# Gated attention followed by two MLP layers on one core: gate sums taken from their middle, masks on a row's last part, row sums in pairs, and one decoding step on another engine

## The chip, the core and the metric

The kernel runs on one core of one Trainium2 chip. The engines are named as the profile names them: PE (matrix products; PEld is its weight load), DVE (vector), ACT (scalar functions), POOL (a third elementwise engine) and SP, whose queue issues all the DMA transfers of this kernel. Each engine works through its own instructions in the order written for it, and waits for others on semaphores. The metric is the device time of one execution in microseconds.

## The reference

Three layers in a row, all in float32:

```python
batch, n_heads, seq, head_dim = (4, 8, 576, 64)
scores = scale * np.matmul(q, k.transpose(0, 1, 3, 2))        # scale = 1/8
causal = np.triu(np.ones((S, S), dtype=bool), k=1)
cum = np.cumsum(np.maximum(s, 0.0), axis=-1)
bias = -(cum[:, :, :, None] - cum[:, :, None, :])
scores = np.where(causal, -1000000000.0, scores + np.minimum(bias, 0.0))
scores = scores - np.max(scores, axis=-1, keepdims=True)
attn = np.exp(scores)
attn = attn / (np.sum(attn, axis=-1, keepdims=True) + 1e-09)
out = np.matmul(attn, v)
...
x = out as [2304, 512]
x = (silu(x @ w_gate) * (x @ w_val)) @ w_out      # 512 -> 1536 -> 512
x = silu(x @ w_in) @ w_out2                       # 512 -> 2048 -> 512
```

A row's softmax doesn't change when a constant is added to the whole row, so of the bias only the part that depends on the key (`cum` at the key) matters to the result.

## The kernel before

**Attention.** There are 32 heads (4 batches of 8). A head's 576 queries are cut into five row tiles, `TILES`, of 64, 128, 128, 128 and 128 rows; a tile's scores reach from key 0 to its last query, so they are 64, 192, 320, 448 and 576 wide. Tiles 0 to 2 are half "A" of a head, tiles 3 and 4 half "B", and a half is a unit. `a_load` issues a head's transfers (`qkr` holds q and k, `cumb` the head's gate sums on all 128 partitions, `vra` and `vrb` the values). `a_split` cuts q and k into a rounded high part (`ks`, `qh`, by `copy`, whose engine letters stand in the strings `KHI` and `QHI`, one letter for each batch: a is ACT, v is DVE, g is POOL) and a remainder (`ql` and the lower rows of `ks`). `a_scores` handles one row tile: POOL writes the gate term into the tile `e` (a `tensor_scalar` over the whole width, L218, then a mask on the diagonal block, `affine_select`, L221), PE makes the scores in PSUM, DVE adds them to `e` and finds the row minimum (`m`, L235), ACT takes the exponential with the row sum `l` (L241), DVE makes `rl` = 1/(l + 1e-9) (L245, L246), and the row is multiplied with it (a `copy`, L114 on DVE or L116 on POOL). `a_transpose` turns the finished rows on PE and `a_pv` multiplies them with the values. There are six `e` tiles, two `cumb` tiles, and five raw weight tiles.

**First MLP layer.** `gate` and `down` work on weight chunks of 2048 columns, nine a batch in the list `L1`. Each product is made three times (`mm3`: high by high, high by low, low by high), so a chunk is 96 matmuls of 288 columns. Weights come as 64-bit words. In the first batch's nine chunks, and in the second layer's eight, `w_decode` has to turn them back to float32, four pieces of 128x512 a chunk: ACT scales the high word (L374), DVE turns the low word to three bits (L375), joins them (L376) and puts the sign in (L379). Later batches read the float32 copy that the first stored. `w_split` then cuts the weights in two parts (`wh` on ACT, `wl` on POOL or DVE, L395).

**Order.** Eighteen units of attention run first, without MLP work, with one chunk's loading and decoding after the ninth. Then the four batches of layer 1 run one after the other, and two units of the next batch's attention are interleaved with each chunk, so that batch 1's attention runs beside batch 0's chunks, while these are being decoded. The fourth batch has no attention beside it. Layer 2 follows. `w_ahead` decodes and splits chunk c+1, and loads chunk c+2, at the start of chunk c. Program order is written so; a scheduler then settles the order on each engine.

## Time and profile before

| | |
|---|---|
| median of 3 runs | 1140.44 us (1138.94 to 1141.12) |
| profiled execution | 1141.18 us, its span 1139.4 us |
| granted PE clock, mean | 0.988 of full speed |
| PE busy | 1096.2 us (96%) |
| DVE busy | 764.8 us (67%) |
| POOL busy | 615.9 us (54%) |
| ACT busy | 561.0 us (49%) |

The span runs from the first to the last instruction; 1.8 us of the execution's time lie outside it. The busy shares are means over stages that differ: the first 76 us are attention alone, then come the four passes of layer 1 (about 76 to 288, 288 to 454, 454 to 615 and 615 to 734 us, read from the first and last matmuls into `pgv` and `po`), then layer 2. Engines take their work in order, so what matters in a stage is the engine that the others wait for there.

### The profile page before, as it was taken

What the parts mean: (1) busy time and instruction counts of PE and PEld (TensorE: products, weight loads), DVE (VectorE), ACT (ScalarE), POOL (GpSimd) and SP (SyncE); (2) the same over time, 40 slices, a digit from 0 to 9 for tenths busy, and PEclk for the clock granted to TensorE, in tenths of its full rate; (3) what the DMA queues carried; (4) which work ended last, traced back from release to release, by engine and by line L of the source; (5) the groups of instructions that cost most, each with busy time, mean ns of one, the idle gap of its engine ahead of it and who ended that gap; (6) DMA issues with size and microseconds to landing.
All of it is one profiled execution on the core that took longest, in us unless ns stands there. A gap on an engine that the chain in (4) does not pass through costs nothing.

```text
span 1139.4 us, 19549 instructions
## 1 busy us (share of the span) xinstructions
PE 1096.2 (96%) x6765; PEld 1000.2 (88%) x6765; DVE 764.8 (67%) x1776; ACT 561.0 (49%) x1242; POOL 615.9 (54%) x731
## 2 busy tenths in 40 slices
PE   7978988989999999999999999999999999999998
PEld 4656888888999999999999999889888898988887
DVE  6888998998877786777766435863463636454333
ACT  5876666655667655576744433455232323322221
POOL 4679889868877776686833543332333232223221
PEclk9988999999999999999999999999999999999999
DMA  5586565666343344333216222630111101000013
GB/s 141 136 244 215 175 193 189 182 173 196 119 119 113 109 117 144 113 101 101 69 54 217 75 84 84 202 109 25 50 51 43 57 19 56 19 1 1 1 51 116
DMA packets 53730, 121.41 MB, mean 107 GB/s; under 512 B 8256, under 2 KB 21568, under 8 KB 53632
## 3 DMA queue, kind: packets, MB, share of 16 engines
q1 hardware_dynamic: 53632, 120.17, 34.6%
q8 instruction: 53, 0.87, 0.3%
q14 instruction: 45, 0.37, 0.1%
HBM read 101.20 MB, written 18.95 MB: 105 GB/s over the span
## 4 chain that ended last, share of the span: by engine, by line
PE 73%; DVE 6%; DMA 2%; issue 2%; ACT 1%; POOL 0%; SPq 0%; DVEq 0%; ACTq 0%
PE po L406 9%; PE po L407 9%; PE po L408 9%; PE pgv L406 7%; PE pgv L407 7%; PE pgv L408 7%; PE pu L407 5%; PE pu L406 5%; PE pu L408 5%; PE pv L292 4%; PE ptr L264 3%; PE psc L230 2%; DVE dk L376 1%; DMA r<-in_w_dram 1%; DMA x2r<-x_d 1%
## 5 line engine op out<-in xcount | busy, mean ns | idle before, releaser
L421 POOL TENSOR_TENSOR h<-u,h 128x288 fp32r<-128x288 f32 (+2 forms) x176 | 187.1, 1064 | 332.5 <-ACT h L112 329.1
L406 PE MATMUL pgv<-xt,wh 128*128 128x288 f32 x768 | 233.7, 305 | 5.0 <-DVE u L417 3.5
L406 PE MATMUL po<-h,wh 128*128 128x288 f32 (+2 forms) x704 | 233.1, 333 | 3.7 <-DVE u L419 1.5
L407 PE MATMUL po<-h,wh 128*128 128x288 f32 (+2 forms) x704 | 232.6, 331 | 0.1
L408 PE MATMUL po<-h,wl 128*128 128x288 f32 (+2 forms) x704 | 232.3, 330 | 0.0
L408 PE MATMUL pgv<-xt,wl 128*128 128x288 f32 x768 | 230.0, 300 | 1.4 <-POOL wl L395 1.4
L407 PE MATMUL pgv<-xt,wh 128*128 128x288 f32 x768 | 230.0, 300 | 0.5 <-DVE xt L313 0.5
L395 POOL TENSOR_TENSOR wl<-wraw,wh 128x1024 fp32r<-128x1024 f32 x53 | 130.0, 2453 | 60.4 <-ACT wh L112 59.9
L406 PEld LDWEIGHTS pgv<-xt,wh 128*128 128x128 f32 x768 | 147.2, 192 | 6.7 <-DVE u L417 4.5
L408 PEld LDWEIGHTS pgv<-xt,wl 128*128 128x128 f32 x768 | 146.7, 191 | 1.8 <-POOL wl L395 1.8
L407 PEld LDWEIGHTS pgv<-xt,wh 128*128 128x128 f32 x768 | 147.1, 192 | 1.1 <-DVE xt L313 0.8
L218 POOL TENSOR_SCALAR e<-cumb,cumq 64x64 f32<-64x64 f32 (+4 forms) x160 | 112.4, 708 | 62.8 <-PE ptr L264 55.2
L406 PEld LDWEIGHTS po<-h,wh 128*128 128x128 f32 x704 | 132.0, 188 | 12.0 <-DVE u L419 2.0
L112 ACT ACTIVATE h<-u 128x288 fp32r<-128x288 f32 (+2 forms) x176 | 88.8, 508 | 102.2 <-DVE u L417 58.5
L408 PEld LDWEIGHTS po<-h,wl 128*128 128x128 f32 x704 | 132.2, 188 | 7.1
L407 PEld LDWEIGHTS po<-h,wh 128*128 128x128 f32 x704 | 132.2, 188 | 6.8 <-POOL h L421 0.5
L241 ACT ACTIVATE e<-e,m 64x64 f32<-64x64 f32 (+4 forms) x160 | 89.2, 558 | 95.9 <-DVE m L235 95.4
L417 DVE SCALAR_TENSOR_TENSOR u<-th,pu 128x464 f32<-128x464 f32 (+1 forms) x80 | 50.5, 631 | 122.3 <-ACT th L415 116.7
L501 DVE SCALAR_TENSOR_TENSOR acc<-po,acc 128x464 f32<-128x464 f32 (+1 forms) x140 | 88.7, 635 | 62.1 <-PE po L408 61.6
L415 ACT ACTIVATE th<-pu 128x464 f32<-128x464 f32 (+1 forms) x80 | 44.2, 552 | 174.0 <-PE pu L408 174.0
L112 ACT ACTIVATE wh<-wraw 128x1024 fp32r<-128x1024 f32 x88 | 92.2, 1053 | 56.0 <-PE po L407 32.1
L407 PE MATMUL pu<-x,wh 128*128 128x464 f32 (+1 forms) x320 | 118.9, 372 | 0.0
(83 smaller groups left out, 2189.3 us busy)
## 6 DMA issues: line engine op xcount, KB each, us to landing
wraw<-w SPq DMA_DIRECT2D x54, 512.0 KB, 4.0
r<-in_w_dram SPq DMA_DIRECT2D x52, 512.0 KB, 5.1
qkr<-in_qk_dram SPq DMA_DIRECT2D x64, 288.0 KB, 4.5
w<-wraw SPq DMA_DIRECT2D x18, 512.0 KB, 4.4
cumb<-cum_d SPq DMA_DIRECT2D x30, 288.0 KB, 3.4
r<-in_w_dram SPq DMA_DIRECT2D x32, 256.0 KB, 3.2
x_d<-acc SPq DMA_DIRECT2D x32, 144.0 KB, 3.8
vrb<-in_vb_dram SPq DMA_DIRECT2D x32, 128.0 KB, 3.6
```

What stands on the lines that cost most here:

```text
L112: nc.scalar.activation(out=out, in_=in_, func=AF.Copy, scale=scale)
L218: nc.gpsimd.tensor_scalar(out=e[:r, :wd], in0=c[:r, :wd], scalar1=-1.0, scalar2=cumq[:r, i, hh : hh + 1], op0=ALU.mult, op1=ALU.add)
L241: nc.scalar.activation(out=e[:r, :wd], in_=e[:r, :wd], func=AF.Exp, bias=m[:r], scale=-1.0, accum_out=l[:r])
L292: nc.tensor.matmul(out=acc[:rows, off : off + width], lhsT=vv, rhs=pp, start=(j == 0 and part == 0), stop=(j == js[-1] and part == len(ps) ...
L395: engines[eng].tensor_tensor(out=wl, in0=t, in1=wh.bitcast(F32), op=ALU.subtract)
L406: nc.tensor.matmul(out=ps[:, :n], lhsT=a, rhs=xh, start=(k == 0), stop=False)
L407: nc.tensor.matmul(out=ps[:, :n], lhsT=a, rhs=xl, start=False, stop=False)
L408: nc.tensor.matmul(out=ps[:, :n], lhsT=c, rhs=xh, start=False, stop=(k == last))
L415: nc.scalar.activation(out=th[:, :n], in_=pg[:, :n], func=AF.Tanh, scale=0.5)
L417: nc.vector.scalar_tensor_tensor(out=u, in0=th[:, :n], scalar=1.0, in1=pg[:, :n], op0=ALU.add, op1=ALU.mult)
L421: engines[LO[ph]].tensor_tensor(out=lo, in0=u, in1=hi.bitcast(F32), op=ALU.subtract)
L501: nc.vector.scalar_tensor_tensor(out=a, in0=ps[:, :n], scalar=0.5, in1=a, op0=ALU.mult, op1=ALU.add)
```

## The change

1. The gate sums are no longer differenced by query. `cum` is centred on the sum at position 288 (`mid`) and multiplied by 8 once; the scores are now made from unscaled q, and L231 multiplies them by -0.125 while it adds the gate. The five transposes and copies to `cumq` at the start are gone.
2. POOL writes no gate term over the whole width any more. It only masks, straight from `cumb`, the part from column `g0` on: all of the row for widths up to 320, and the last 128 or 256 columns of the wider ones. DVE reads the part before `g0` from `cumb` itself. So the tile of width 448 has two DVE additions (320 and 128) instead of one, and the tile of 576 is cut into 320 and 256 instead of 288 and 288.
3. The row sums of tiles 1 and 2, and of tiles 3 and 4, lie in two columns of one tile; 1e-9 and the reciprocal are done once for both, after the second.
4. All rows are now scaled on POOL (`DVE_NORM` is gone; it had put tiles 0, 1 and 3 of batch 0 on DVE).
5. In batch 0, `qh` is made on DVE, not ACT, `ql` on POOL, not DVE, and one of the copies of transposed rows (128x384, half B) moves from ACT to DVE.
6. In `w_decode`, the low word's conversion moves from DVE (L375) to ACT (a second `activation` that writes `dk`).

```diff
+POOL_QL = (0,)
-DVE_PT = ()
+DVE_PT = (("B", 3),)
-QHI = "aavv"
+QHI = "vavv"
-DVE_NORM = [(0, i) for i in (0, 1, 3)]
...
+        mid = sm_p.tile([B * H, 1], F32, tag="m", name="mid")
+        nc.vector.tensor_copy(out=mid, in_=cum[:, HB : HB + 1])
+        nc.vector.tensor_scalar(out=cum, in0=cum, scalar1=mid, scalar2=8.0, op0=ALU.subtract, op1=ALU.mult)
         nc.sync.dma_start(out=cum_d, in_=cum)
-        for i, (q0, r) in enumerate(TILES):
-            pt = ps_a.tile([P, 512], F32, tag="a", name=f"pcum{i}")
-            nc.tensor.transpose(pt[:r, : B * H], cum[:, q0 : q0 + r], ident[: B * H, : B * H])
-            nc.vector.tensor_copy(out=cumq[:r, i, :], in_=pt[:r, : B * H])
...
-            copy(QHI[b], qh[:, q0:k1], t[:, 0, q0:k1], -0.125)
+            copy(QHI[b], qh[:, q0:k1], t[:, 0, q0:k1])
...
-            nc.vector.scalar_tensor_tensor(
-                out=ql[:, q0:k1], in0=t[:, 0, q0:k1], scalar=-0.125, in1=qh[:, q0:k1].bitcast(F32),
-                op0=ALU.mult, op1=ALU.subtract,
-            )
+            eng = nc.gpsimd if b in POOL_QL else nc.vector
+            eng.tensor_tensor(out=ql[:, q0:k1], in0=t[:, 0, q0:k1], in1=qh[:, q0:k1].bitcast(F32), op=ALU.subtract)
...
-        nc.gpsimd.tensor_scalar(
-            out=e[:r, :wd], in0=c[:r, :wd], scalar1=-1.0, scalar2=cumq[:r, i, hh : hh + 1], op0=ALU.mult, op1=ALU.add
+
+        g0 = 0 if wd <= 320 else 320
+        nc.gpsimd.affine_select(
+            out=e[:r, g0:wd], in_=c[:r, g0:wd], pattern=[[-1, wd - g0]], compare_op=ALU.is_ge,
+            fill=-8.0 * QMASK, base=q0 - g0, channel_multiplier=1,
         )
...
+            for g, end, gate in ((c0, min(g0, c0 + n), c), (max(g0, c0), c0 + n, e)):
+                if g >= end:
+                    continue
+                m2 = sm_p.tile([P, 1], F32, tag="m", name="m")
+                nc.vector.tensor_tensor_reduce(
+                    out=e[:r, g:end], in0=ps[:r, g - c0 : end - c0], in1=gate[:r, g:end], scale=-0.125,
+                    scalar=3.0e38 if m is None else m[:r], op0=ALU.add, op1=ALU.min, accum_out=m2[:r],
+                )
+                m = m2
...
-        copy("v" if (b, i) in DVE_NORM else "g", e[:r, :wd], e[:r, :wd], rl[:r])
         st[b, h, "e", i] = e
+        if i in (1, 3):
+            return
+        done = (0,) if i == 0 else (i - 1, i)
+        w = len(done)
+        rl = sm_p.tile([P, 2], F32, tag="rl", name="rl")
+        nc.vector.tensor_scalar(out=l[:r, :w], in0=l[:r, :w], scalar1=1.0e-9, scalar2=None, op0=ALU.add)
+        nc.vector.reciprocal(out=rl[:r, :w], in_=l[:r, :w])
+        for n, j in enumerate(done):
+            q0, r = TILES[j]
+            e = st[b, h, "e", j]
+            copy("g", e[:r, : q0 + r], e[:r, : q0 + r], rl[:r, n : n + 1])
...
-            nc.vector.tensor_scalar(out=k, in0=lo, scalar1=2.0**-29, scalar2=7.0, op0=ALU.mult, op1=ALU.min)
+            nc.scalar.activation(out=k, in_=lo, func=AF.Copy, scale=0.937 * 2.0**-29)
```

The start on DVE, before, from the last copy to `cumq` to the first addition of scores (`ISA e,m`):

```order
L143 COPY cumq<-pcum_146 128x32
L193 TENSOR_TENSOR ks<-qkr,ks 64x576
L194 SCALAR_TENSOR_TENSOR ql<-qkr,qh 128x576
L193 TENSOR_TENSOR ks<-qkr,ks 64x576
L194 SCALAR_TENSOR_TENSOR ql<-qkr,qh 128x576
L235 ISA e,m<-psc,e 64x64
```

The same place with the change:

```order
L141 COPY mid<-cum 32x1
L142 TENSOR_SCALAR cum<-cum,mid 32x576
L114 TENSOR_SCALAR qh<-qkr 128x576
L191 TENSOR_TENSOR ks<-qkr,ks 64x576
L114 TENSOR_SCALAR qh<-qkr 128x576
L191 TENSOR_TENSOR ks<-qkr,ks 64x576
L231 ISA e,m<-psc,e 64x64
```

Two `ql` have gone to POOL, two `qh` have come from ACT, and the five copies have given way to two operations on `cum`.

On ACT, in the middle of the first pass, before: the decoding of one chunk of weights (r is a piece as it came from memory) between attention (e, ph, xtmp, qh, ks) and gating (th, h):

```order
L374 ACTIVATE wraw<-r_2262 128x512
L374 ACTIVATE wraw<-r_2264 128x512
L112 ACTIVATE qh<-qkr 128x576
L112 ACTIVATE ks<-qkr 128x576
L374 ACTIVATE wraw<-r_2266 128x512
L374 ACTIVATE wraw<-r_2268 128x512
L306 ACTIVATE xtmp<-pv 64x256
L273 ACTIVATE ph<-ptr 64x320
L415 ACTIVATE th<-pgv 128x288
```

With the change, the first half of such a chunk (L381 is the old L374, L382 the conversion that came from DVE):

```order
L382 ACTIVATE dk<-r_2128 128x512
L112 ACTIVATE wh<-wraw 128x1024
L382 ACTIVATE dk<-r_2130 128x512
L422 ACTIVATE th<-pgv 128x288
L241 ACTIVATE e,l<-e,m 128x448
L112 ACTIVATE h<-u 128x288
L112 ACTIVATE qh<-qkr 128x576
L112 ACTIVATE ks<-qkr 128x576
L241 ACTIVATE e,l<-e,m 128x576
L112 ACTIVATE h<-u 128x288
L381 ACTIVATE wraw<-r_2128 128x512
L381 ACTIVATE wraw<-r_2130 128x512
```

The conversions of a chunk's first two pieces stand some ten instructions ahead of their L381, right behind the arrival of the pieces; exponentials (L241) and the gating's `th` (L422) are queued behind them.

On DVE, the same first half of a chunk, before:

```order
L375 TENSOR_SCALAR dk<-r_2264 128x512
L235 ISA e,m<-psc,e 128x448
L235 ISA m 128x1
L274 TENSOR_TENSOR pl<-ptr,ph 64x256
L419 TENSOR_TENSOR u<-pgv,u 128x288
L274 TENSOR_TENSOR pl<-ptr,ph 128x512
L274 TENSOR_TENSOR pl<-ptr,ph 128x384
L245 TENSOR_SCALAR l<-l 128x1
L246 RECIPROCAL rl<-l 128x1
L376 SCALAR_TENSOR_TENSOR dk<-wraw,dk 128x512 x2
L235 ISA e,m<-psc,e 128x288
```

With the change:

```order
L231 ISA e,m<-psc,e 64x64
L231 ISA m 64x1
L199 TENSOR_TENSOR vsa<-vra,vsa 64x64
L383 SCALAR_TENSOR_TENSOR dk<-wraw,dk 128x512 x2
L314 TENSOR_TENSOR x<-pv,xtmp 64x256
L386 SCALAR_TENSOR_TENSOR wraw<-r_2128,dk 128x512
L281 TENSOR_TENSOR pl<-ptr,ph 64x320
L386 SCALAR_TENSOR_TENSOR wraw<-r_2130,dk 128x512
L281 TENSOR_TENSOR pl<-ptr,ph 128x384
```

The joining (L383) and the sign (L386) are left on DVE, and no conversion stands between them and attention's additions.

## Rows read from the trace of the kernel before

**Rows 1.** Busy time by stage: engines (instructions), PE clock, DMA share, GB/s.

```profile
0.00:76.00 76.00, 63.42 (x304) 40.88 (x304) 57.91 (x218) 57.31 (x153) 45.36 (x96) 0.98 0.60 162
76.00:288.00 212.00, 188.59 (x1262) 172.09 (x1263) 194.51 (x470) 126.78 (x295) 179.30 (x211) 0.94 0.65 192
288.00:454.00 166.00, 166.00 (x1231) 158.67 (x1230) 131.40 (x361) 102.75 (x254) 125.92 (x170) 1.00 0.40 120
...
734.00:1139.00 405.00, 401.55 (x1920) 359.77 (x1918) 196.30 (x307) 130.16 (x226) 116.22 (x87) 1.00 0.14 47
```

**Rows 2.** PE's waits, 76 to 288 us: total, times, longest.

```profile
PE psc L230 <- DVE m L235: 4.4, 3, 2.9
...
PE pgv L406 <- DVE u L417: 3.0, 3, 2.2
```

**Rows 3.** The chain that ended last: start us, us, what.

```profile
193.92 2.73 DVE dk L376
...
230.10 5.12 DMA r<-in_w_dram
...
717.62 2.59 DVE dk L375
```

**Rows 4.** DVE's groups, 76 to 288 us: busy us, mean ns, idle before.

```profile
L376 DVE SCALAR_TENSOR_TENSOR dk<-wraw,dk 128x512 uint32<-128x512 uint32 x33 | 38.7, 1186 | 3.0 <-ACT wraw L374 3.0
L379 DVE SCALAR_TENSOR_TENSOR wraw<-r,dk 128x512 uint32<-128x512 uint32 x34 | 32.1, 948 | 0.1
...
L375 DVE TENSOR_SCALAR dk<-r 128x512 uint32<-128x512 uint32 x32 | 20.5, 642 | 4.6 <-DMA r<-in_w_dram 4.6
...
L419 DVE TENSOR_TENSOR u<-pgv,u 128x288 f32<-128x288 f32 x24 | 10.6, 443 | 0.0
...
L246 DVE RECIPROCAL rl<-l 128x1 f32<-128x1 f32 (+1 forms) x49 | 7.0, 151 | 0.5
```

**Rows 5.** The same stretch and engine, shapes kept apart.

```profile
L235 DVE CUSTOM_DVE_ANT_0 e<-psc,e 128x448 f32<-128x448 f32 x10 | 6.1, 611 | 0.4 <-PE po L407 0.2 <-PE psc L230 0.2
...
L235 DVE CUSTOM_DVE_ANT_0 e<-psc,e 128x320 f32<-128x320 f32 x10 | 4.8, 478 | 0.0
...
L114 DVE TENSOR_SCALAR e<-e,rl 128x192 f32<-128x192 f32 x1 | 2.4, 2361 | 0.0
...
L114 DVE TENSOR_SCALAR qh<-qkr 128x576 fp32r<-128x576 f32 x2 | 0.9, 459 | 0.0
```

**Rows 6.** DVE's groups, 0 to 76 us.

```profile
L379 DVE SCALAR_TENSOR_TENSOR wraw<-r,dk 128x512 uint32<-128x512 uint32 x3 | 2.2, 736 | 0.0
L376 DVE SCALAR_TENSOR_TENSOR dk<-wraw,dk 128x512 uint32<-128x512 uint32 x3 | 2.1, 703 | 0.0
```

**Rows 7.** POOL's groups, 76 to 288 us.

```profile
L395 POOL TENSOR_TENSOR wl<-wraw,wh 128x1024 fp32r<-128x1024 f32 x19 | 47.1, 2476 | 3.1 <-ACT wh L112 3.0
L218 POOL TENSOR_SCALAR e<-cumb,cumq 128x448 f32<-128x448 f32 (+4 forms) x48 | 35.2, 737 | 5.8 <-PE ptr L264 5.4
...
L221 POOL TENSOR_SCALAR_AFFINE_SELECT e<-e 128x128 f32<-128x128 f32 (+1 forms) x49 | 22.5, 473 | 0.0
```

**Rows 8.** ACT's groups, 76 to 288 us.

```profile
L374 ACT ACTIVATE wraw<-r 128x512 f32<-128x512 f32 x32 | 19.8, 668 | 8.8 <-issue 4.1 <-DMA w<-wraw 1.9 <-DVE wraw L379 1.2
```

**Rows 9.** The start in order of time, ACT and DVE: start us, us.

```profile
9.95 0.68 ACT L112 ACTIVATE ks<-qkr 128x576 fp32r<-128x576 f32 x1 [1.44 <-DMA qkr<-in_qk_dram]
...
10.67 2.25 DVE L193 TENSOR_TENSOR ks<-qkr,ks 64x576 fp32r<-64x576 f32 x1 [1.75 <-ACT ks L112]
...
13.62 0.21 DVE L235 CUSTOM_DVE_ANT_0 e<-psc,e 64x64 f32<-64x64 f32 x1
```

**Rows 10.** A slice of the stage of attention alone, columns as in the first group.

```profile
40.00:50.00 10.00, 9.70 (x55) 6.33 (x53) 7.55 (x33) 9.04 (x25) 7.24 (x17) 1.00 0.41 108
```

**Rows 11.** DVE's groups, 288 to 454 us.

```profile
L114 DVE TENSOR_SCALAR qh<-qkr 128x576 fp32r<-128x576 f32 x9 | 12.7, 1413 | 0.1
```

**Rows 12.** Longest waits of SP's queue, 0 to 300 us: total, times, longest.

```profile
SPq L170 <- POOL e L218: 40.1, 12, 5.8
```

More of the change, by code (lines that the diff above doesn't have):

```diff
@@ L121 @@
     cum = const.tile([B * H, S], F32, name="cum")
-    cumq = const.tile([P, len(TILES), B * H], F32, name="cumq")
     cum_d = dram.tile([B * H, S], F32, name="cum_d")
@@ L182, in a_split @@
             ks, qs = t[:D, 1], (t[:D, 0],)
-            q = t[:D, 0, q0:k1]
-            nc.vector.tensor_scalar(out=q, in0=q, scalar1=-0.125, scalar2=None, op0=ALU.mult)
         else:
@@ L215, in a_scores @@
         wd = q0 + r
-        hh = b * H + h
         e = e_p.tile([P, S], F32, tag="e", name="e")
-        nc.gpsimd.tensor_scalar(
-            out=e[:r, :wd], in0=c[:r, :wd], scalar1=-1.0, scalar2=cumq[:r, i, hh : hh + 1], op0=ALU.mult, op1=ALU.add
-        )
-        nc.gpsimd.affine_select(
-            out=e[:r, q0:wd], in_=e[:r, q0:wd], pattern=[[-1, r]], compare_op=ALU.is_ge,
-            fill=QMASK, base=0, channel_multiplier=1,
-        )
-        chunks = [(0, wd)] if wd <= 512 else [(0, wd // 2), (wd // 2, wd // 2)]
+        g0 = 0 if wd <= 320 else 320
+        nc.gpsimd.affine_select(
+            out=e[:r, g0:wd], in_=c[:r, g0:wd], pattern=[[-1, wd - g0]], compare_op=ALU.is_ge,
+            fill=-8.0 * QMASK, base=q0 - g0, channel_multiplier=1,
+        )
         m = None
-        for c0, n in chunks:
+        for c0, n in ((0, wd),) if wd <= 512 else ((0, g0), (g0, wd - g0)):
             ps = ps_a.tile([P, 512], F32, tag="a", name="psc")
@@ L233, in a_scores @@
                 )
-            m2 = sm_p.tile([P, 1], F32, tag="m", name="m")
-            nc.vector.tensor_tensor_reduce(
-                out=e[:r, c0 : c0 + n], in0=ps[:r, :n], in1=e[:r, c0 : c0 + n], scale=1.0,
-                scalar=3.0e38 if m is None else m[:r], op0=ALU.add, op1=ALU.min, accum_out=m2[:r],
-            )
-            m = m2
-        l = sm_p.tile([P, 1], F32, tag="l", name="l")
+            for g, end, gate in ((c0, min(g0, c0 + n), c), (max(g0, c0), c0 + n, e)):
[7 more added lines that the diff above has]
+                m = m2
+        if i in (0, 1, 3):
+            st[b, h, "l"] = sm_p.tile([P, 2], F32, tag="l", name="l")
+        l = st[b, h, "l"]
+        col = 1 if i in (2, 4) else 0
         nc.scalar.activation(
-            out=e[:r, :wd], in_=e[:r, :wd], func=AF.Exp, bias=m[:r], scale=-1.0, accum_out=l[:r]
+            out=e[:r, :wd], in_=e[:r, :wd], func=AF.Exp, bias=m[:r], scale=-1.0, accum_out=l[:r, col : col + 1]
         )
-        rl = sm_p.tile([P, 1], F32, tag="rl", name="rl")
-        nc.vector.tensor_scalar(out=l[:r], in0=l[:r], scalar1=1.0e-9, scalar2=None, op0=ALU.add)
-        nc.vector.reciprocal(out=rl[:r], in_=l[:r])
-        copy("v" if (b, i) in DVE_NORM else "g", e[:r, :wd], e[:r, :wd], rl[:r])
         st[b, h, "e", i] = e
+        if i in (1, 3):
[9 more added lines that the diff above has]
+            copy("g", e[:r, : q0 + r], e[:r, : q0 + r], rl[:r, n : n + 1])
     def a_transpose(b, h, half, js):
```

## The prediction

> **What bounds the kernel now.** I first cut the span into stages and read the busy times of each [rows 1]. From 288 us on PE is busy all the time (166.00 of 166 us in the second pass), so nothing that DVE, ACT or POOL saves there can shorten anything; in layer 2 PE lacks 3.45 of 405 us. The exception is the first pass, 76 to 288 us: PE is busy for 188.59 of 212 us and got a mean clock of 0.94, and DVE is busy for 194.51, or 92%. The second pass holds nearly the same products (1231 matmuls against 1262) and takes 166 us. So the first pass is 46 us longer than its matrix work, and those 46 us are what can be won. Which engine holds it back shows in PE's waits there: all the large ones end on DVE, on the row minimum and on the gating [rows 2]. And the chain that ended last runs, early on, over single decoding operations of DVE, one of 2.73 us [rows 3].
>
> Why such an operation takes 2.7 us shows when its group is compared between stages. Joining the bits (L376) takes 1186 ns in the first pass [rows 4] and 703 ns before it, beside a lighter POOL [rows 6]; the sign (L379) 948 against 736 ns. POOL is busy for 179.30 of the 212 us [rows 1], much of it with operations of 2476 ns (L395) [rows 7]. The gating product L419, whose one input is in PSUM, takes 443 ns in the pass with the busy POOL [rows 4]. So what DVE does from SBUF alone waits for POOL's operations, and the bound of the pass is DVE plus the part of POOL that blocks it.
>
> The stage before, 0 to 76 us, is different: between 40 and 50 us PE is busy 9.70 of 10 us, ACT 9.04, DVE 7.55 [rows 10]. It is bound by PE, with ACT just behind.
>
> **The change, part by part.**
>
> *The conversion L375.* 32 of its operations lie in the first pass, 20.5 us at 642 ns each [rows 4]. Records of neighbours overlap (an operation at 13.62 us lasts 0.21 us, beyond the start of its successor in that view), so I take 18 us off DVE; the bounds are 13 us (32 at some 400 ns, the length that the 459 ns of the single-input `qh` [rows 5] gives for 512 columns) and 25 us, if the 4.6 us of waiting for the pieces' arrival [rows 4] go too. On ACT each has to be paid: L374, of the same shape and stride, takes 668 ns [rows 8], so 32 cost 21 us. ACT is busy 126.78 of 212 us [rows 1]; with that, some 147 of 187 us. It hides, as long as ACT does not stand still in front of it.
>
> Against this step stands a rule of the Trainium skill (ScalarE: Activation LUTs, Rules for kernel authors): multiplications belong on VectorE, which is the faster engine for them. By it the kernel would lose the difference between the two durations. In the rows the two lie close, 668 against 642 ns, as DVE's figure includes its waiting for POOL; and ACT has idle time in this pass and DVE has none, so by the rows the sum keeps its 18 us, and by the rule it would keep 17.
>
> *Row sums by twos.* A head has three pairs of L245 and L246 instead of five. In the pass 49 of each [rows 4] become 29. Twenty reciprocals of 151 ns and as many additions, taken as equally long, are 6 us by their records; back to back they take about half that, and I take 3 (bounds 1.5 and 6).
>
> *The split additions.* Width 448 took 611 ns, 320 takes 478 [rows 5]; that is 1.04 ns a column, so 128 columns are 278 ns, an estimate. One more addition for each of ten heads is 10 x (478 + 278 - 611) = 1.5 us, and one more short read of the minimum makes it 2 us more on DVE (bounds 1.5 and 3). Width 576 keeps two additions. PE's columns stay the same (448 once, 576 in two).
>
> *The norms of batch 0* leave DVE. What is left of them in the pass is mainly one operation that took 2361 ns [rows 5]: 2.4 us.
>
> *POOL's gate work.* Before, L218 takes 35.2 us and L221 22.5 us in the pass [rows 7], 58 together. Now there is one mask a tile, over 64, 192, 320, 128 and 256 columns. The trace shows no wider mask than 128. From below, 48 of them at the 473 ns of L221 are 23 us; from above, at the 737 ns of L218, 35 us. I take 29, nearer to L221 for the narrow ones and to L218 for the wide ones. POOL sheds 29 of 179 us, a sixth. DVE's waiting for POOL in L376 and L379 is 33 x 483 + 34 x 212 ns = 23 us; a sixth of it is 4 us (bounds 0, if only the 2476 ns of L395 block, and 8, if the other two-input operations gain alike).
>
> On this bears the Trainium skill (SBUF — State Buffer, Who interferes with whom): a DVE instruction with two SBUF inputs, or in a two-port mode, and a GpSimd instruction that reads SBUF exclude each other for their whole length; one with a PSUM input is spared. The groups agree: 1186 against 703 ns, and 443 ns for L419. By that rule the new `qh` on DVE in batch 0 would be blocked too, and the rows have such a case: 1413 ns in the second pass [rows 11] against 459 [rows 5]. Eight of them, blocked, are 8 x 0.95 = 7.6 us more on DVE in the first stage. That is busy 57.91 of 76 us there, so I expect it hidden; if none were, the sum below would fall from 32 to 24.
>
> The first pass: 18 + 3 + 2.4 + 4 - 2 = 25 us off DVE's 194.5. If DVE stays at its 92% or a little under, the pass takes 187 us instead of 212. The bounds are 7 (ACT stands in DVE's place) and 46 (the 166 us of PE).
>
> *The start and batch 0's attention.* Before, the first addition of scores stands behind two `ql` and a `ks` that took 2.25 us, and comes at 13.62 us [rows 9]. Now `qh` and `ks` of the second head are ahead of it; its q and k have landed by 9.95 us, so 0.46 + 0.76 us later, at 11.2 us, it can run (at 12.7 us if `ks` is blocked again). That is 1 to 2.4 us. `mid` and the centring cost DVE less than the five transposes and copies that they replace. After that PE can be closed up by 3% of some 46 us, 1.4 us. ACT is relieved of `qh` and a copy; POOL takes `ql` and three norms a head and sheds its gate term, and has room, 45.36 of 76 us [rows 1]. I take 4 us in all (bounds 0 and 7).
>
> *Layer 2.* The conversion stands on the end's chain there too: once for 2.59 us, at 717.62 us [rows 3], and a few times for under half of that. Off DVE it is 0.67 us on ACT. I take 3 us (bounds 0 and 4).
>
> *Nothing* from: the `cumq` tile, the unscaled q, passes two to four. One wait is moved: DVE now reads `cumb` at its additions, later than POOL did, and SP's reload of `cumb` (L170) already waits 40.1 us in 12 cases [rows 12]; behind it in SP's queue stand the values and the weight pieces. A delay of 1 to 2 us there eats from prefetch; I cost it at nothing, and it belongs to the third case below.
>
> Sum: 25 + 4 + 3 = 32 us. From the profiled execution's 1141.18 us that is 1109.2; its time lies 0.74 us above the median of the three runs, so against that median 1108.5.
>
> **The rivals.**
>
> *PE becomes the bound of the whole first pass.* For it: DVE would be at 169 us of work and PE needs 166, and the clock of 0.94 [rows 1] would rise with fewer gaps. Then 46 + 7 + 4 = 57 us go and the time is 1084. Against it: before, DVE was at 92% and PE at 89% of the same pass, and neither closed up; two engines that wait for each other left gaps in both.
>
> *The decoding stays a chain.* Both conversions of a piece are now ACT's, and L376 waited for ACT already (3.0 us [rows 4]); L383 then waits where L375 once worked. If the decoding gives nothing, 7 of the 25 us are left, and 7 + 3 + 1 = 11 us give 1130; if half of it, 1120.
>
> *ACT is stopped by the transfers: slower.* The first two conversions of each chunk stand ahead of exponentials and `th`, right where a piece must land; one landing on the chain took 5.12 us [rows 3]. Eight chunks that each wait a whole landing with PE's next inputs behind are 41 us, and the time is 1140.4 - 32 + 41 = 1149. It decides from 4 us a chunk on. Against it: DVE waited only 4.6 us in all for the same pieces in 32 conversions [rows 4].
>
> **How the numbers follow.** The forecast gets 0.68, with a range of its own of 1100 to 1117; PE as the bound 0.12; the decoding as a chain 0.12; ACT stopped 0.08, of which a quarter ends near no change. The predicted time is 1108. The range 1086 to 1128 leaves out half of the first rival, most of the last and the far end of the second, under 2 in 10. A measurement of this kernel tells 0.2%, 2.3 us, from no change: faster 0.92, same 0.02, slower 0.06.
>
> **What would show it.** Right: in the profile after, the first pass (first `pgv` to the last `po` of batch 0) takes 180 to 190 us, with DVE still near 90% busy and POOL under 155 us; the conversion on ACT takes 0.65 to 0.7 us; passes two to four are unchanged to 2 us; the first addition comes between 11 and 13 us. Wrong: ACT's waits for weight pieces over 15 us in the first pass, or PE waiting for `th` and exponentials; L383 waiting for ACT's conversion over 10 us; or a first stage over 76 us, with `qh` on DVE near 1.4 us.

## The result and the profile after

The changed kernel took 1128.24 us (median of 4 runs, 1125.41 to 1129.1) beside 1140.78 us for the kernel before: ratio 0.9888, interval 0.9866 to 0.991. Run again later it took 1125.66 us (1124.7 to 1129.58), ratio 0.987 (0.9852 to 0.9887). It is faster, by 12.5 to 15 us instead of the 32 that were forecast.

Lengths of the stages in the profiled executions, read from the same matmuls into `pgv` and `po` in each trace (us):

| | until first `pgv` | first pass | its end | second | third | fourth | layer 2 | span |
|---|---|---|---|---|---|---|---|---|
| before | 76.0 | 212.3 | 288.3 | 165.8 | 161.2 | 118.3 | 405.8 | 1139.4 |
| before, again | 75.5 | 213.7 | 289.3 | 165.8 | 161.2 | 119.3 | 405.1 | 1140.7 |
| changed | 80.7 | 197.3 | 278.0 | 163.0 | 161.0 | 118.2 | 407.0 | 1127.2 |
| changed, again | 79.8 | 197.4 | 277.2 | 163.0 | 161.0 | 115.1 | 406.8 | 1123.1 |

Two profiles of one program agree within 1.4 us up to the third pass; the fourth of the changed kernel differs by 3. Of the 15 us that the first pass won, the stage ahead of it gave 4 to 5 back. The second pass's 2.8 us is work moved forward: it holds 1212 matmuls now [rows 1: 1231], the first pass 1275 instead of 1262.

The windows of the changed kernel, one row a stage (columns: window, length, then busy time of each engine with its count, granted clock, DMA share, GB/s):

```profile
core 0: us, PE busy (x) PEld busy (x) DVE busy (x) ACT busy (x) POOL busy (x), PEclk, DMA share, GB/s
...
0.00:81.00 81.00, 66.05 (x306) 42.75 (x307) 59.07 (x193) 56.05 (x148) 49.90 (x91) 0.95 0.62 162
81.00:278.00 197.00, 183.74 (x1275) 167.54 (x1274) 171.83 (x421) 143.54 (x330) 164.06 (x168) 0.98 0.68 206
278.00:441.00 163.00, 163.00 (x1212) 156.43 (x1211) 126.39 (x329) 98.03 (x243) 99.88 (x121) 1.00 0.42 118
720.00:1127.00 407.00, 401.95 (x1924) 360.10 (x1923) 188.84 (x284) 144.41 (x250) 114.11 (x87) 1.00 0.15 48
```

In the first pass DVE's busy time fell from 194.51 to 171.83 us, by 22.7 where the forecast's sum said 25. But the pass did not follow at DVE's old share of 92%: the share is 87%. PE's waits in it (81 to 278 us), after those of [rows 2]:

```profile
engine line waited for: us in total, times, longest us
PE ptr L271 <- POOL e L116: 5.9, 7, 1.4
PE psc L223 <- DVE x L314: 1.8, 2, 0.9
PE psc L223 <- DVE pl L281: 1.4, 1, 1.4
```

The large waits on DVE's row minimum and gating have shrunk (4.4 to 1.0 us and 3.0 to 0.7 us in total). The largest is now the transposes' wait for rows that POOL scales; the rest is spread thinly. DVE's groups there:

```profile
L386 DVE SCALAR_TENSOR_TENSOR wraw<-r,dk 128x512 uint32<-128x512 uint32 x32 | 25.2, 788 | 0.1
L383 DVE SCALAR_TENSOR_TENSOR dk<-wraw,dk 128x512 uint32<-128x512 uint32 x32 | 23.9, 759 | 0.5 <-ACT dk L382 0.2 <-ACT wraw L381 0.2
...
L193 DVE TENSOR_TENSOR ql<-qkr,qh 128x576 fp32r<-128x576 f32 x10 | 16.8, 1680 | 3.2 <-ACT qh L112 3.2
L250 DVE TENSOR_SCALAR l<-l 128x2 f32<-128x2 f32 (+1 forms) x28 | 13.9, 497 | 2.0 <-ACT e L241 2.0
...
L320 DVE TENSOR_TENSOR xt<-x,xt 128x320 fp32r<-128x320 f32 (+1 forms) x10 | 5.4, 544 | 0.5 <-ACT xt L112 0.5
...
L251 DVE RECIPROCAL rl<-l 128x2 f32<-128x2 f32 (+1 forms) x28 | 4.3, 154 | 0.4
```

Beside [rows 4], joining takes 759 instead of 1186 ns and the sign 788 instead of 948: the two operations got some 18 us shorter, not 4. Joining is preceded by 0.5 us of waiting in all, 0.2 of it for ACT's conversion, so the decoding did not stay a chain. What gave much of this back is L250, the addition of 1e-9, now over two columns: 497 ns on average, where a reciprocal of the same shape takes 154. The timeline shows how, in one case (start, duration):

```profile
137.90 3.30 DVE L250 TENSOR_SCALAR l<-l 128x2 f32<-128x2 f32 x1
...
138.04 0.80 POOL L428 TENSOR_TENSOR h<-u,h 128x288 fp32r<-128x288 f32 x1
...
138.80 2.37 POOL L402 TENSOR_TENSOR wl<-wraw,wh 128x1024 fp32r<-128x1024 f32 x1
```

An addition of two numbers a partition ended only when two POOL operations had ended (141.17 us). By the Trainium skill (VectorE: DVE Perf Modes, Mode 2×_2P, and SBUF — State Buffer, Who interferes with whom), a one-source DVE operation from SBUF to SBUF whose outermost non-unit dimension is even can use both ports, and in that mode it and GpSimd exclude each other. The trace agrees on that: the additions over 128x2 wait, those over 128x1, which have no such dimension, don't (at most 157 ns in any trace). It does not agree on the order: the section has the operation go first that was issued first, and by the records these two POOL operations started after the addition (a mask of POOL's was still running then).

POOL's group of scaled rows in the first pass of the kernel before, then POOL's and ACT's groups in that of the changed kernel:

```profile
L116 POOL TENSOR_SCALAR e<-e,rl 128x576 f32<-128x576 f32 (+4 forms) x46 | 32.4, 709 | 9.8 <-DVE rl L246 6.8 <-ACT e L241 2.4 <-ACT wh L112 0.5
```

```profile
L402 POOL TENSOR_TENSOR wl<-wraw,wh 128x1024 fp32r<-128x1024 f32 x19 | 47.1, 2483 | 3.6 <-ACT wh L112 3.5
L116 POOL TENSOR_SCALAR e<-e,rl 128x192 f32<-128x192 f32 (+4 forms) x49 | 40.6, 838 | 7.0 <-DVE rl L251 4.9 <-PE psc L223 2.1
L215 POOL TENSOR_SCALAR_AFFINE_SELECT e<-cumb 128x256 f32<-128x256 f32 (+4 forms) x50 | 30.8, 636 | 7.1 <-PE ptr L271 6.7
```

```profile
L382 ACT ACTIVATE dk<-r 128x512 uint32<-128x512 uint32 x32 | 21.3, 668 | 5.2 <-DMA r<-in_w_dram 5.1
```

The masks cost 30.8 us (estimated 29) and the conversion 668 ns each (as estimated). POOL as a whole is busy for 164.06 us, not under 155: scaling the rows takes 40.6 us now instead of 32.4. At the start, on DVE (start, duration, idle before):

```profile
9.61 0.52 DVE L114 TENSOR_SCALAR qh<-qkr 128x576 fp32r<-128x576 f32 x1 [0.67 <-DMA qkr<-in_qk_dram]
10.32 2.32 DVE L191 TENSOR_TENSOR ks<-qkr,ks 64x576 fp32r<-64x576 f32 x1 [0.19 <-ACT ks L112]
12.66 0.22 DVE L231 CUSTOM_DVE_ANT_0 e<-psc,e 64x64 f32<-64x64 f32 x1
...
17.82 1.11 DVE L250 TENSOR_SCALAR l<-l 128x2 f32<-128x2 f32 x1
```

The first addition comes at 12.66 us instead of 13.62 [rows 9], but the lead is gone by the first product with values (19.6 us, before 19.5). In layer 2 ACT waits for pieces (690 to 1127 us):

```profile
ACT dk L382 <- DMA r<-in_w_dram: 21.1, 8, 4.9
```

### The profile page after: what moved, and what is told of

Its sections match the earlier page's. It is cut to its first block, busy times and chain, and to the rows that moved or that the text cites. A ratio compares the mean times of both kernels' runs of the same rounds, so it can differ in the third digit from the quotient of the medians.

```text
span 1127.2 us, 19389 instructions
## 1 busy us (share of the span) xinstructions
PE 1091.4 (97%) x6760; PEld 996.5 (88%) x6760; DVE 726.0 (64%) x1625; ACT 589.3 (52%) x1294; POOL 562.7 (50%) x603
## 5 line engine op out<-in xcount | busy, mean ns | idle before, releaser
L428 POOL TENSOR_TENSOR h<-u,h 128x288 fp32r<-128x288 f32 (+2 forms) x176 | 192.7, 1096 | 341.0 <-ACT h L112 338.7
L116 POOL TENSOR_SCALAR e<-e,rl 64x64 f32<-64x64 f32 (+4 forms) x160 | 101.9, 647 | 57.6 <-DVE rl L251 42.5
L422 ACT ACTIVATE th<-pu 128x464 f32<-128x464 f32 (+1 forms) x80 | 44.1, 551 | 151.2 <-PE pu L415 151.2
L241 ACT ACTIVATE e<-e,m 64x64 f32<-64x64 f32 (+4 forms) x160 | 89.1, 557 | 56.9 <-DVE m L231 55.9
```

The lines of the kernel that those rows point to most:

```text
L116: nc.gpsimd.tensor_scalar(out=out, in0=in_, scalar1=scale, scalar2=1.0, op0=ALU.mult, op1=ALU.mult)
L241: nc.scalar.activation(out=e[:r, :wd], in_=e[:r, :wd], func=AF.Exp, bias=m[:r], scale=-1.0, accum_out=l[:r, col : col + 1])
L422: nc.scalar.activation(out=th[:, :n], in_=pg[:, :n], func=AF.Tanh, scale=0.5)
L428: engines[LO[ph]].tensor_tensor(out=lo, in0=u, in1=hi.bitcast(F32), op=ALU.subtract)
```

## The experiments

Kernels named `a_` start from the changed kernel, those named `b_` from the kernel before. Each is compared with the kernel before on its own chip.

| kernel | median us | ratio, interval | end of first pass | first pass | lane |
|---|---|---|---|---|---|
| before | 1140.78 | 1 | 288.3 | 212 | 221 |
| `b_sums_by_twos` | 1146.93 | 1.0047 (1.003 to 1.0064) | 298.0 | 223 | 228 |
| `b_dk_on_act` | 1138.34 | 0.9969 (0.9957 to 0.9982) | 289.7 | 210 | 210 |
| `b_gate_only` | 1134.05 | 0.9933 (0.9917 to 0.995) | 285.7 | 211 | 202 |
| `b_dk_and_gate` | 1124.86 | 0.986 (0.9845 to 0.9875) | 276.4 | 201 | 188 |
| changed | 1128.24 | 0.9888 (0.9866 to 0.991) | 278.0 | 197 | 190 |
| `a_dk_on_dve` | 1141.14 | 1.0003 (0.9992 to 1.0014) | 293.2 | 215 | 208 |
| `a_one_column` | 1123.83 | 0.9848 (0.9834 to 0.9863) | 275.6 | 197 | 187 |
| `a_batch0_back` | 1126.23 | 0.9868 (0.9851 to 0.9885) | 278.0 | 200 | 190 |
| `a_casts_on_act` | 1128.97 | 0.9898 (0.9882 to 0.9915) | 278.1 | 198 | 185 |
| `a_full_masks` | 1135.83 | 0.9956 (0.9942 to 0.9971) | 287.6 | 207 | 195 |
| `a_no_add` | 1136.14 | 0.9958 (0.9946 to 0.997) | 287.5 | 208 | 187 |
| `a_no_mask` | 1130.3, one run | | 280.5 | 202 | 173 |
| `a_no_conversion` | 1130.07, one run | | 280.9 | 205 | 195 |
| `a_no_sign` | 1133.94, one run | | 286.2 | 211 | 172 |
| `a_all_light` | 1112.12, one run | | 266.0 | 193 | 156 |

The last column, the lane, is worked out: over the first pass, the sum of all POOL operations and of DVE's operations that read SBUF alone, each at its undisturbed length (that of the fastest twentieth of its group over all traces of this case). DVE's operations over one column and the reciprocals are left out, as they wait for nobody. If the two kinds excluded each other at all times, the pass could not be much shorter than this sum (records overlap a little, so it may read some per cent high).

**Parts of the change on the kernel before.** The conversion alone:

```diff
-nc.vector.tensor_scalar(out=k, in0=lo, scalar1=2.0**-29, scalar2=7.0, op0=ALU.mult, op1=ALU.min)
+nc.scalar.activation(out=k, in_=lo, func=AF.Copy, scale=0.937 * 2.0**-29)
```

> The kernel before with the conversion of the low word on ACT and nothing else. Theory of the prediction: 14 to 20 us less, 1121 to 1127 us, all of it in the first pass. Rival, that the decoding stays a chain: 1136 to 1141 us. If it alone gives 1127 or less, the rest of the change together gives nothing or costs.

It gained 3 us, with the end of the first pass where it was; the second pass is 2.7 us shorter. The time lies in the rival's range, but not by its mechanism: the join waits 0.2 us in all here. Its windows row for the first pass:

```profile
80.00:290.00 210.00, 189.70 (x1278) 171.56 (x1278) 183.81 (x449) 147.24 (x335) 184.94 (x215) 0.95 0.63 193
```

DVE went down to 183.81 us from 194.51, POOL up to 184.94 from 179.30. Taking time off DVE alone did not pay.

Parts 1 and 2 alone, then with the conversion (the edits are those of the change):

> The kernel before with only the gate's part of the change: sums from their middle, additions that read them, masks on a row's last part, q unscaled. Two theories. Shared lane: in the first pass GpSimd's operations and DVE's operations that read SBUF alone exclude each other, so that what counts is the sum of the two at undisturbed lengths; this edit takes some 20 us of GpSimd's and gives back a few on DVE (ql 1680 against 1198 ns, the third addition), so the first pass falls by 8 to 14 us, to 1127 to 1132 us in all. Rival, two bounds: DVE's own time (194 of 212 us) holds the pass, and GpSimd comes second; then GpSimd's relief alone gives 0 to 4 us and the time is 1137 to 1143 us, as moving the conversion alone gave 3.

> The gate's part and the conversion on ACT together, without the row sums by twos and without batch 0's moves. Shared lane: the conversion and the gate's part add up, and since neither the two-column addition nor batch 0's moves cost anything here, 1116 to 1122 us. Rival, two bounds: each of them alone gives 0 to 4 us and both together some 17, so 1120 to 1126 us. If the parts left out are what gains, 1128 us or more.

The gate's part gave 7.5 us: 1134.05 us lies between the ranges of the two theories, and the first pass won only 1.6 us of it, not the 8 to 14 of the shared lane; 2.8 are the second pass's moved matmuls. With POOL relieved, DVE's waiting moved to the conversion, 1032 instead of 642 ns, and DVE stayed as busy as before (75 to 286 us, windows row and two of DVE's groups):

```profile
75.00:286.00 211.00, 190.40 (x1286) 172.67 (x1286) 198.31 (x504) 130.47 (x304) 158.32 (x165) 0.95 0.64 195
L373 DVE TENSOR_SCALAR dk<-r 128x512 uint32<-128x512 uint32 x32 | 33.0, 1032 | 1.0 <-DMA r<-in_w_dram 0.9
L374 DVE SCALAR_TENSOR_TENSOR dk<-wraw,dk 128x512 uint32<-128x512 uint32 x33 | 28.3, 866 | 1.4 <-ACT wraw L372 1.4
```

Gate and conversion together gave 16.7, more than 3 and 7.5 added. The time, 1124.86 us, lies in the rival's range and not in that of the shared lane. The gate and the conversion alone do at least as well as the whole change; parts 3 to 5 cost or bring nothing.

Row sums by twos alone (`l` is 128x2, with a column for each tile of a pair):

```diff
...
-        nc.vector.tensor_scalar(out=l[:r], in0=l[:r], scalar1=1.0e-9, scalar2=None, op0=ALU.add)
-        nc.vector.reciprocal(out=rl[:r], in_=l[:r])
+        nc.vector.tensor_scalar(out=l[:r, :w], in0=l[:r, :w], scalar1=1.0e-9, scalar2=None, op0=ALU.add)
+        nc.vector.reciprocal(out=rl[:r, :w], in_=l[:r, :w])
```

> The kernel before with only the row sums by twos (addition and reciprocal over two columns, two norms behind each other). Theory, from the changed kernel's rows: the two-column addition waits for GpSimd, 19 x (667 - 2 x 140) = 7 us more on DVE in the first pass where DVE is busy for 92%; 1144 to 1150 us. Rival, the prediction's own: fewer instructions, 2 to 4 us less, 1136 to 1139 us.

It is slower, by 5.9 us, as expected of a blocked addition: the group takes 12.5 us, where 49 additions of one column took 6.8. (Joining, with POOL not relieved, went down to 880 ns here; so the 18 us above are not all POOL's relief.) DVE's groups of this kernel, 75 to 298 us:

```profile
L253 DVE TENSOR_SCALAR l<-l 128x2 f32<-128x2 f32 (+1 forms) x30 | 12.5, 417 | 1.1 <-ACT e L244 0.7
...
L254 DVE RECIPROCAL rl<-l 128x2 f32<-128x2 f32 (+1 forms) x30 | 4.5, 152 | 0.2
```

**Parts taken back in the changed kernel.** `a_dk_on_dve` has the diff above reversed.

> The changed kernel with the conversion of the low word back on DVE, in its old form. Theory of the prediction: its move is worth some 18 us of DVE time in the first pass, so undoing it gives 1140 to 1148 us. Rival, that the decoding stays a chain and ACT's share of it costs as much as DVE gained: 1125 to 1132 us, no change to the changed kernel; and layer 2 gets shorter by a few us, as ACT no longer waits there for pieces in front of its other work.

The whole gain is gone, and the first pass is 17 us longer. Its windows row there, with DVE at 93% again:

```profile
78.00:293.00 215.00, 189.53 (x1281) 172.57 (x1282) 200.82 (x458) 130.19 (x303) 163.01 (x171) 0.95 0.63 189
```

So the conversion's move is worth 13 us where POOL has been relieved (9 between `b_gate_only` and `b_dk_and_gate`), and 3 where it has not. Layer 2 was 2.4 us shorter with it on DVE, and the fourth pass 1.0 longer than the changed kernel's (4.1 longer than its repeat's).

```diff
-        nc.vector.tensor_scalar(out=l[:r, :w], in0=l[:r, :w], scalar1=1.0e-9, scalar2=None, op0=ALU.add)
+        for n in range(w):
+            nc.vector.tensor_scalar(
+                out=l[:r, n : n + 1], in0=l[:r, n : n + 1], scalar1=1.0e-9, scalar2=None, op0=ALU.add
+            )
```

> The changed kernel, with the 1e-9 added to each column of the row sums by an instruction of its own; the reciprocal still takes two columns. Theory: the addition over two columns is held up by GpSimd's operations (667 ns mean in the first pass, longest 3304 ns) and an addition over one column is not (140 ns, longest 156 before). Then the groups of the addition fall to about 140 ns, DVE loses 19 x (667 - 2 x 140) = 7 us in the first pass, and the time falls from 1128 to 1119 to 1123 us. Rival: the first pass is held by other things (ACT's conversion, TensorE's waits for the norms); then the group falls alike, but the time stays at 1126 to 1130 us.

1123.83 us lies between the two expected ranges; it is level with `a_one_col_dk_late` below as the fastest, and its interval overlaps that of the changed kernel's repeat. The group fell to 142 ns, longest 154, as expected, but the first pass stayed at 197.2 us. DVE's groups there, beside those of the changed kernel above:

```profile
L389 DVE SCALAR_TENSOR_TENSOR wraw<-r,dk 128x512 uint32<-128x512 uint32 x32 | 27.9, 875 | 0.0
L386 DVE SCALAR_TENSOR_TENSOR dk<-wraw,dk 128x512 uint32<-128x512 uint32 x32 | 25.5, 810 | 0.9 <-ACT dk L385 0.6 <-ACT wraw L384 0.2
...
L323 DVE TENSOR_TENSOR xt<-x,xt 128x320 fp32r<-128x320 f32 (+1 forms) x10 | 9.0, 900 | 0.5 <-ACT xt L112 0.5
...
L251 DVE TENSOR_SCALAR l<-l 128x1 f32<-128x1 f32 (+1 forms) x47 | 6.7, 142 | 6.4 <-ACT e L241 6.3
```

The addition lost 7.2 us (13.9 to 6.7); the two decoding operations and `xt` got 7.9 us longer. The waiting for POOL seems to have been handed to DVE's next operations. What was won stands ahead of the pass: the first product with values comes at 17.9 us instead of 19.6.

> The changed kernel with batch 0's work back on its old engines: qh of the first two heads on ACT, ql on DVE, three norms of a head on DVE, the one transposed probability tile back on ACT. Theory: the first stage (0 to 81 us) gained nothing since this part costs 2 to 5 us there, with ks blocked on DVE (1602 ns) and norms behind the blocked additions; then the time falls to 1123 to 1126 us. Rival: the part is worth the 2 to 4 us of the prediction, and something else took them; then 1130 to 1133 us.

```diff
-POOL_QL = (0,)
-DVE_PT = (("B", 3),)
-QHI = "vavv"
+POOL_QL = ()
+DVE_PT = ()
+QHI = "aavv"
+DVE_NORM = [(0, i) for i in (0, 1, 3)]
...
```

The first pass ends at 278.0 us as in the changed kernel: what is won at the start (2.2 us) is lost in the pass. Batch 0's moves are worth nothing either way.

**Work added, moved and left out.** `a_casts_on_act` sets `VHI = "aaaa"`; `a_full_masks` masks `e[:r, :wd]` instead of `e[:r, g0:wd]`; `a_no_mask` drops the mask, `a_no_conversion` ACT's second operation, `a_no_sign` DVE's L386, `a_all_light` all three. The last four were timed once each.

> The changed kernel with the two roundings of the values on ACT instead of GpSimd for batch 1 too: GpSimd loses 10 us of its 164 in the first pass, ACT gets some 5 us. Shared lane: the first pass falls by 4 to 10 us, to 1118 to 1124 us. Rival (TensorE or ACT holds the pass by now): 1126 to 1130 us, or more if ACT's exponentials come later.

> The changed kernel with every mask over the whole row instead of its last part (448 columns instead of 128, 576 instead of 256; the additions overwrite the rest, the result is the same). GpSimd gets some 18 to 20 us more in the first pass, DVE, ACT and TensorE nothing. Shared lane: DVE's operations that read SBUF alone grow longer with it and the first pass grows by 10 to 18 us, to 1138 to 1146 us in all. Rival: GpSimd, idle for 33 of 197 us, takes it in and TensorE stays the bound; 1127 to 1132 us.

> The changed kernel without the masks (every addition reads the plain sums; rows see later columns too). GpSimd loses 31 us of its 164 in the first pass (81 to 278 us). Shared lane: DVE's blocked operations get shorter and the first pass falls by 8 to 15 us, to 182 to 189 us. Rival, TensorE and its chains hold the pass by now: 193 us or more.

> The changed kernel without the conversion of the low word (the join on DVE stands, and reads the high word's tile twice, so the weights' low bits are wrong). ACT loses 21 us of its 143 in the first pass, DVE keeps its work. If ACT's place in the chain (conversion before join, exponentials behind it) holds the pass, it falls by 8 us or more, below 189 us. If ACT's part is hidden as the prediction had it: 195 to 198 us, and layer 2 still 2 to 3 us shorter.

> The changed kernel without the second of DVE's two operations a piece, the one that puts the sign back (weights lose their signs). DVE loses 25 us of its 172 in the first pass (81 to 278 us), ACT and GpSimd nothing. If DVE still holds the pass, it falls by 10 us or more from 197, to 187 us or less. If TensorE's own work and order hold it, it stays at 193 us or more.

> The changed kernel without masks, without the conversion on ACT and without the sign's operation (output wrong in all three): 31 us less on GpSimd, 21 on ACT, 25 on DVE in the first pass. If the three engines hold the pass only together, it comes near TensorE's floor, an estimate of 174 to 182 us (the second pass takes 163 us for 1209 of its matmuls, the first has 1273 and some time at half clock). If TensorE's order holds it: 192 us or more.

With more masks the kernel is 7.6 us slower, 1135.83 us, between the ranges of its two theories. But taking work off gave nothing: with 10 us of casts less on POOL the first pass ends where it did (278.1 us), with the masks gone and POOL busy for 33 us less 2.5 us later, without the conversion 2.9 us later, and without the sign, with DVE relieved of 25 us, 8 us later. Only with all three out does it end earlier, by 12 us, 7 of which were won ahead of the pass. Windows rows of the passes of `a_no_mask`, `a_no_sign` and `a_all_light`:

```profile
78.00:280.00 202.00, 185.87 (x1273) 169.50 (x1272) 170.87 (x421) 142.87 (x331) 131.32 (x118) 0.96 0.66 202
75.00:286.00 211.00, 192.94 (x1283) 175.05 (x1282) 156.27 (x395) 147.38 (x342) 145.41 (x169) 0.94 0.64 198
73.00:266.00 193.00, 183.93 (x1287) 169.85 (x1288) 159.86 (x399) 131.48 (x312) 129.30 (x121) 0.97 0.73 220
```

No engine but PE is above 85% busy in any of them. Another thing changed in all of them: the scheduler sorts each program anew. The next experiment shows it best. It drops the addition altogether; its beginning on PE against the changed kernel's (- changed, + `a_no_add`, where L270 is the changed kernel's L271):

```
 L223 MATMUL psc<-ks,qh 64x64
 L223 MATMUL psc<-ks,ql 64x64
+L270 MATMUL ptr<-ident,e 64x128
+L270 MATMUL ptr<-ident,e 128x128 x2
 L223 MATMUL psc<-ks,qh 128x192
 L223 MATMUL psc<-ks,ql 128x192
-L271 MATMUL ptr<-ident,e 64x128
-L271 MATMUL ptr<-ident,e 128x128 x2
```

> The changed kernel without the addition of 1e-9 (a row's sum is at least 1, so that in float32 nothing changes). If the blocked addition is what costs, the time is that of the column-by-column version or a little less, 1121 to 1124 us, with start and first pass together 3 to 5 us shorter. If the wait for GpSimd is only handed on to DVE's next operation and the earlier gain was chance, 1126 to 1129 us.

> The changed kernel once more, unchanged. If its stages are its own: 1127 to 1130 us, the first pass within 2 us of 197, its end within 2 us of 278. If one profile's stages scatter by more than that, differences of 2 to 3 us between the variants' stages can't be read.

With less work on DVE it is 8 to 10 us slower than the changed kernel, against both expectations, while the changed kernel itself repeats its stages. From that place on the sequence differs again and again, on every engine: of DVE's 1529 instructions other than the additions 132 have left their place in it, of ACT's 1294 103. In the repeat none has. DVE's groups of `a_no_add`, 78 to 288 us:

```profile
L382 DVE SCALAR_TENSOR_TENSOR dk<-wraw,dk 128x512 uint32<-128x512 uint32 x33 | 28.6, 877 | 1.6 <-ACT wraw L380 1.1 <-ACT dk L381 0.3
L385 DVE SCALAR_TENSOR_TENSOR wraw<-r,dk 128x512 uint32<-128x512 uint32 x33 | 28.6, 872 | 0.1
...
L193 DVE TENSOR_TENSOR ql<-qkr,qh 128x576 fp32r<-128x576 f32 x10 | 18.6, 1861 | 9.1 <-ACT qh L112 9.1
```

The 14 us of additions are hardly seen in DVE's total (170.51 us in 80 to 287.5, against 171.83): by their means the join and the sign took 6 to 7 of them, `ql` 2. How the pass got longer can be read on PE, from the windows of the pass and of two stretches in it:

```profile
80.00:287.50 207.50, 190.24 (x1273) 172.65 (x1272) 170.51 (x395) 143.55 (x330) 156.95 (x166) 0.93 0.65 194
184.00:192.00 8.00, 8.00 (x62) 7.57 (x61) 3.58 (x11) 6.39 (x12) 3.73 (x3) 1.00 0.59 215
...
197.20:205.00 7.80, 7.80 (x31) 7.12 (x32) 7.34 (x22) 5.83 (x16) 2.45 (x4) 0.50 0.50 153
```

Of the 10 us, 4 are more idle time (17 us against 13) and 6.5 more busy time for as many matmuls (190.24 us for 1273 against 183.74 for 1275). The busy time goes with the granted clock, 0.93 against 0.98. Between the two stretches PE waited 4.39 us for DVE (up to 197.07 us), which had spent 4.47 us on one `ql`, its work from SBUF alone, while POOL was busy; in the wait the clock fell to 0.50, the lower of its two levels (1.2 of 2.4 GHz), and the next 7.80 us held 31 matmuls, where 8.00 us ahead of the wait held 62. So one late handover cost more here than its own length. Differences of up to some 10 us between variants of the changed kernel can't be put down to the edited operation. No neutral edit of the kernel before was timed, so how far its variants scatter is open.

> The kernel before once more, unchanged, for the scatter of its stages. Every variant so far has a second pass of 163.0 to 163.1 us, the kernel before 165.8 in its profile. If that is chance, this run shows 163 us and other stages within 2 us of the first profile; if it belongs to the old code, 165 to 166 us again.

The second pass is 165.8 us again, so its 2.8 us belong to the old code's order.

**Layer 2 and a mix.** `a_one_col_dk_late` adds a choice by chunk to `a_one_column`; `a_best_mix` undoes batch 0's moves as well.

```diff
-            nc.scalar.activation(out=k, in_=lo, func=AF.Copy, scale=0.937 * 2.0**-29)
+            if c < len(stream) - 6:
+                nc.scalar.activation(out=k, in_=lo, func=AF.Copy, scale=0.937 * 2.0**-29)
+            else:
+                nc.vector.tensor_scalar(out=k, in0=lo, scalar1=2.0**-29, scalar2=7.0, op0=ALU.mult, op1=ALU.min)
```

> The changed kernel with the 1e-9 added column by column, and with the conversion on ACT only up to the second chunk of layer 2, on DVE for its last six. Theory: layer 2 lost 2 to 3 us since ACT stands waiting for pieces there (404.6 us with the conversion on DVE, 406.5 to 408 without), and the fourth pass gained as much; then both are had, and the time is 1120 to 1122 us against 1123.8 with the addition alone mended. Rival: layer 2 loses at its very start, in chunks that stay on ACT; 1123 to 1126 us.

> The same with batch 0's moves undone as well. Theory: undoing them gave 2 us to the changed kernel, so 1118 to 1120 us. Rival: what they cost at the start is given back in the first pass (78.5 and 199.5 us against 80.7 and 197.3), so no better than the kernel without this, 1120 to 1124 us.

1123.88 us (0.9846, 0.9825 to 0.9867) and 1129.09 us (0.9886, 0.9869 to 0.9903). Layer 2 kept its 407 us, so ACT's waiting for pieces in the last six chunks is not what lengthened it; the rival (a loss at its very start) fits, and its cause stays open. The mix, of changes that each looked neutral or good, is 5 us slower than `a_one_column`, by its first pass (204 us), which is within the scatter of orders.

## Why the prediction was wrong

**What held.** The stage was read rightly: the first pass, with DVE and POOL both in its way. The conversion took 668 ns on ACT and hides there; the masks cost 30.8 us against 29; DVE's busy time fell by 22.7 us against 25; the first addition came at 12.66 us, within 11 to 13; passes three and four kept their length to 2 us in the first profile. PE as the bound of the whole pass, the chain in the decoding and ACT stopped by the transfers did not come (0.2 us of waiting for the conversion, 5.1 us for pieces in the pass). The time fell near the 1130 us of the chain by chance, as its mechanism did not come.

**Where the 32 us went.** Beside the forecast the first pass won 15 us instead of 25, the start lost 4 to 5 instead of winning 4, and layer 2 lost 1 instead of winning 3; the second pass, costed at nothing, won 2.8.

**What failed, first: "If DVE stays at its 92% or a little under, the pass takes 187 us instead of 212."** DVE's time went nearly as summed and the pass won 15, not 25: DVE's share fell to 87%. DVE's busy time contains its waiting for POOL, so it and its share were no bound; with the sign left out DVE was busy for only 156.27 of 211 us (75 to 286). The lane was tried in its place. While it stands at 202 to 228 us, all six passes lie within 9 us of it (212, 214, 223, 210, 211, 215), and the change takes it from 221 to 190. But it does not order those six (a lane of 202 goes with a pass of 211, 221 with 212), from 195 down to 156 the passes lie between 193 and 211 and don't go with it, and the times that it forecast for `b_gate_only`, `b_dk_and_gate`, `a_full_masks` and `a_casts_on_act` and the pass for `a_no_mask` did not come. So it is not shown as the bound either. What holds the passes near 200 us is not one engine's time alone, as leaving out work on POOL, ACT or DVE did not help. An estimate: at the second pass's pace (163.00 us for 1212 matmuls) the first pass's 1275 need 171 us; 13 us of idle PE and 0.02 of clock on 197 us, 4 us, make 188; in the remaining 9 us PE counts as busy, and what they are is not shown. That leaves short waits in many places and the clock after them, as read in `a_no_add`. That the order in which each engine's work stands is the cause was argued from variants that are each sorted anew; no run held the order fixed, so it is not shown, and what sets the length of the pass now stays open.

**Second: "Twenty reciprocals of 151 ns and as many additions ... I take 3."** The sign was wrong. The addition was priced by the reciprocal; over two columns it waits for POOL, 497 ns mean of its group and up to 3.30 us. Alone, the part made the kernel 5.9 us slower. In the changed kernel, mending it gives 2 to 4 us. Both are less than the scatter between orders, so the longer addition is shown, and its price in the kernel's time is not.

**Third, a size: what the two decoding operations gain from POOL's relief, "a sixth of it is 4 us".** The two decoding operations got 18 us shorter (32 x 427 ns and 32 x 160 ns are 13.7 and 5.1). The additions (13.9 us) and `ql` as a two-input operation (1680 ns) took part of that back, so DVE's total came out near the forecast by cancelling errors.

**Fourth: "I take 4 us in all" for the start.** The first addition's gain of 1 us was lost by the first product with values (a two-column addition of 1.11 us is on the way), and the stage up to the first `pgv` got 4 to 5 us longer. The sign named for this came in half: the stage is over 76 us, but its eight `qh` on DVE took 440 to 515 ns, so the 7.6 us priced for blocked ones did not come. Which part lengthened the stage is open: the first `pgv` comes at 80.1 us with the conversion alone, at 75.5 with gate and conversion. With the moves of batch 0 undone nothing changed at the end of the pass: they are worth 0, the lower bound.

**Fifth: layer 2, 3 us.** It got 1.2 us longer. The conversion at 717.62 us [rows 3] belongs to the fourth pass, which gained 0 to 3 us (118.2 and, in the repeat, 115.1 against 118.3 and 119.3); layer 2 lost it at its start (189 matmuls in its first 41 us, before 196).

The conversion and the gate's part make up the gain, and bring more together than alone: 3 us and 7.5 us, then 16.7. That they need each other, since each relieves one side of DVE and POOL, fits `a_dk_on_dve` too, but the 6 us in excess are less than the scatter between orders.

## What to carry to other kernels

Where two engines block each other, don't take either one's busy share as the bound of a stage, and try a change to both sides together before it is judged by one side alone. Busy time that contains waiting is no measure, for what one operation no longer waits the next one will. When a scheduler sorts the program anew after each edit, time an unchanged kernel and a few neutral edits first, and don't read differences under that scatter (here 1 to 3 us a stage for the same order, some 10 us for a new one). Read PE's idle time and its granted clock beside each other, since a wait can cost more than its own length.

## What the hardware showed

Here an addition's shape decided whether it waits for POOL: over 128x2 it took up to 3.30 us and over 128x1 at most 157 ns, while the reciprocal over 128x2 never took more than 168 ns. So merging two tiny instructions into one made them dearer on average than both (667 ns against two of 142, in the first pass).

Taking work from an engine went with a slower kernel more than once: 14 us of additions less, and 8 to 10 us more; 25 us of sign operations less, and some 6 us more in its one run. That the scheduler's new order made them slower is likely and not shown.
